# Neighbourhood attention on one core: where G's first tile, band 2's copies and band 3's loads stand in the order

## The chip, the cores and the metric

The kernel runs on one core of a Trainium2 chip. A core has five engines that each work through a queue of their own in order: TensorE (PE, matrix products into PSUM), VectorE (DVE), ScalarE (ACT), GpSimd (POOL) and SyncE (SP), which issues most of the DMAs. They wait for each other by semaphores. The time is that of one execution on the device, in microseconds; of several runs the median is given.

## The reference, cut to what matters

The image x has 224 x 224 pixels of 192 channels in bf16. Each pixel attends to 49 others: a 7 x 7 grid with a step of two pixels, clipped at the borders of the image.

```python
qkv = x @ wqkv                                   # 192 -> 3 * 192
off = jnp.arange(7) * 2
r0 = jnp.clip(ir - 6, 0, H - 1 - 12); c0 = jnp.clip(ic - 6, 0, W - 1 - 12)
nidx = rows r0 + off, columns c0 + off           # 49 neighbours of each pixel
logits = einsum('bnc,bnkc->bnk', q, k[nidx]) * C ** -0.5
p = softmax(logits)
o = einsum('bnk,bnkc->bnc', p, v[nidx]) @ wo
```

## The kernel before

**Pixels.** Because the step of the grid is two, a pixel meets only rows and columns of its own parity. The rows are handled in 14 steps n, each of one row parity rc and one group ti of 16 rows of it (`steps`, L591), and each step in seven pairs m = 0 to 6 of two slots of 8 columns (`pairs`). So there are 98 pairs, k = 0 to 97. Both column parities (cc) of a slot are done together.

**Algebra.** q and k are not formed. The scores are x times G, where G is x times the product of the two weight matrices (AW); V is x times the product of wv and wo (WP, WB). G and V are made one step ahead: while step n attends, PE makes G and V for step n + 1.

**Input.** x is loaded as 14 bands of 16 image rows. `load_items` (L145) issues three transposing DMAs on SP for one band: channels go to the partitions, two tiles into the rings XA[0] and XA[1], and a third into a tile X1 with 64 rows of either column parity. X1 has two buffers, so X1 of band b takes the buffer of X1 of band b - 2 once all readers of that are done. `xb_items` (L158) copies the halves of X1 into the rings XB[0] and XB[1], whose other 64 partitions hold marks that mask what lies outside of the grid. `sort_items` (L167) copies a band from XA and X1 into XS in the order that V needs. Later bands are copied and sorted by POOL, through the list `pool_q`.

**One pair.** `stage1` multiplies G by the x rows of a slot (PE, L499) into one of two standing PSUM tiles, SS[0] for slot 0 and SS[1] for slot 1, and takes the negative maximum nmx (DVE, L501). `stage1b` makes the exponentials p (ACT, L508), two instructions a slot. `stage2` transposes p (PE, L527; called T below) and copies the result out of PSUM (DVE, L528). `stage3` multiplies by V (PE, L537, into o_ps). `stage4` divides by the sum (DVE, L543 and L560) and stores. The stages of pair k are interleaved with the later stages of pairs k - 1 and k - 2.

**Work for the next step.** For G there are four column groups (`GROUPS`), each with three items (`g_items`): two `whole` tiles, one for each column parity (PE L417, then copied to G by `evac`, on ACT L330), and one `halves` item that goes by ACT to a tile gx and from there by POOL (L452) into G. There are 14 V items (`v_item`: PE L337 and L340, then ACT L330 or DVE L328). All these PSUM tiles come from one pool of three banks (`ps_g`), so a fourth waits until the first is copied out.

**The order.** The order on each engine is that of the program text (`in_order`, L90). In the main loop (L657) a pair emits the scores of both slots, the exponentials of slot 0, stage 3 and the first stage 4 of pair k - 2, then the list `w64`, the exponentials of slot 1, stage 2 of pair k - 1, the second stage 4, one load (`ld.pop`, L700), and the list `w128`. In steps 1 to 12 w64 is a `halves` item in even pairs and empty in odd pairs; w128 holds one `whole` tile (two in pair 1) and two V items. In step 0 the order of this later part is written out by hand in `PLAN` (L606), one string a pair: V is a V item of step 0, W one of step 1, G and H `whole` tiles of steps 0 and 1, X a copy of band 2 into XB, R and T copies of V between its two buffers by DMA (`v_over`), N the second stage 4; a or d behind it names ACT or DVE.

**Around the change in step 0.** `load_items(2)` is issued before the loop (L628). SP then carries, in order, `g_row_on(0, 4, 10)` (L278), a first load of band 3, the v copy R-:0:8, a second load of band 3, R-:8:14, `first_vd` (L366), `g_row_on(1, 2, 12)`, `g_col_on` (L284), the last load of band 3 (X1), and the stores of pairs 2 and on. POOL sorts bands 1 and 2 in pairs 0, 1 and 3 and copies band 3 into XB from pair 4 on.

Of the kernel before, what the change touches and what calls it, by code (L numbers as in the profile page):

```python
# [19 lines left out]
S = 112  # L20
# [3 lines left out]
NBAND = 14  # L24
# [43 lines left out]
def _win(t, p0, pn, off, dims):  # L68
    a = t[:]
    ps = a.ap[0][0]  # L70
    return bass.AP(a.tensor, a.offset + p0 * ps + off, [[ps, pn]] + [list(d) for d in dims])
# [28 lines left out]
def kernel(  # L100
# [7 lines left out]
    nc = tc.nc  # L108
# [19 lines left out]
    XB = [pers.tile([128, RP * RW], BF, name=f"xb{m}") for m in range(2)]  # L128
    XDAT = (0, 64)
# [8 lines left out]
    X1 = {}  # L138
# [6 lines left out]
    def load_items(b):  # L145

        src = xp[16 * b:16 * b + 16].rearrange("r j c -> (r j) c")
        at = (16 * b) % (2 * RP) * S

        def one(k):  # L150
            if k == 1:
                X1[b] = x1_p.tile([128, BND], BF, name=f"x1_{b}", tag="x1")
            dst = X1[b][:] if k == 1 else XA[k // 2][:, at:at + BND]
            nc.sync.dma_start_transpose(out=dst.unsqueeze(1), in_=src[:, 128 * k:128 * k + 128])  # L154

        return [lambda k=k: one(k) for k in ((0, 2, 1) if b in (0, 2, 3) else (1, 0, 2))]

    def xb_items(b, eng):  # L158
        at = (16 * b) % (2 * RP) * S
        return [lambda m=m: eng(out=XB[m][XDAT[m]:XDAT[m] + 64, at:at + BND], in_=X1[b][XDAT[m]:XDAT[m] + 64, :]) for m in range(2)]  # L160
# [45 lines left out]
    for cc in range(2):  # L206
        t = pers.tile([128, S], BF, name=f"ch{cc}")
        at = (S - KS) % MM if cc else 0
# [65 lines left out]
    def g_row_on(rc, s0, ns):  # L274

        for cc in range(2):
            p = XROW[cc]
            nc.sync.dma_start(out=_win(G[rc][cc], p, 32, (NSLOT + s0) * 128, [[128, ns], [1, 128]]), in_=_win(G[rc][cc], p, 32, (NSLOT + 1) * 128, [[0, ns], [1, 128]]))  # L278
# [63 lines left out]
    def v_item(rc, ti, cb):  # L342
        def emit(dve):
            pv = ps_g.tile([128, 512], F32, name="pv", tag="pg")
            v_mms(pv, lambda k, h: XS[rc][:, k, cb, 64 * h:64 * h + 64])
            evac(_win(VV[rc][ti % 2], 0, 128, AT[cb] * VP, [[193, 2], [1, C]]), pv[:, 0:2 * C].rearrange("p (t c) -> p t c", c=C), dve)
        return emit

    def v_over(rc, ti, c0, c1, eng=nc.sync):

        eng.dma_start(out=VV[rc][1 - ti % 2][0:64, c0:c1, 0:VP - 1], in_=VV[rc][ti % 2][0:64, c0:c1, 0:VP - 1])
# [153 lines left out]
    def stage1b(J, ab):  # L505
        s_ps, nmx = J.s[ab]
        for cc in range(2):
            nc.scalar.activation(out=J.p[:, ab, cc].rearrange("p q (r k) -> p q r k", k=8), in_=_win(s_ps, 0, 128, cc * 256, [[8, 2], [16, 16], [1, 8]]),  # L508
                                 func=ACTF.Exp, bias=nmx[:, cc:cc + 1], scale=1.0)
# [20 lines left out]
    def stage3(J, ab):  # L530
        rc, s = J.rc, 2 * J.m + ab
        o_ps = (ps_o if J.k < NP - 1 else ps_g).tile([128, 512], F32, name="o_ps", tag="o" if J.k < NP - 1 else "pg")
        V = (VV[rc][1 - J.ti % 2], VV[rc][J.ti % 2])
        for cc in range(2):
            for q in range(2):
                for h in range(2):
                    nc.tensor.matmul(o_ps[64 * h:64 * h + 64, cc * 193:cc * 193 + 193], lhsT=J.pt[:, 4 * ab + 2 * cc + q, 64 * h:64 * h + 64],  # L537
                                     rhs=V[h][:, AT[(s - 1 + q) % NSLOT], cc * C:cc * C + 193], start=(q == 0), stop=(q == 1))
        J.o_ps[ab] = o_ps

    def stage4a(J, ab):
        J.rs[ab] = stat.tile([128, 2], F32, name="rs", tag="rs")
        nc.vector.reciprocal(out=J.rs[ab][:], in_=J.o_ps[ab][:, C:C + 2])  # L543
        return J.rs[ab]
# [55 lines left out]
    def g_all(n):  # L600
        ti, rc = steps[n]
        its = [g_items(rc, ti, s0, ns) for (s0, ns) in GROUPS]
        return [it for (w0, w1, h) in its for it in (w0, w1)], [h for (w0, w1, h) in its]

    act, dve, pool = nc.scalar.copy, nc.vector.tensor_copy, nc.gpsimd.tensor_copy
    PLAN = (  # L606
        "Va:0 Vd:1 Va:2 Vd:3 Va:4 Vd:5 Va:6 Vd:7 R-:0:8 Va:8 Gd:2 Ga:3 X-",
        "Va:9 Vd:10 X- Va:11 Vd:12 Va:13 R-:8:14 Gd:4 Ga:5",
        "Gd:6 N- Ga:7 Wa:0 Wd:1 Wa:2",
        "Hd:0 N- Ha:1 Wa:3 Wa:4 Wd:5",  # L610
        "Hd:2 N- Ha:3 Wa:6 Wa:7 Ta:0:8 Wd:8",
# [37 lines left out]
    g_row(1, 0, 0, 1, pool, first1)  # L649
    g_row(1, 0, 1, 1, pool, first1)  # L650
    g_row_on(0, 4, 10)
    xb2 = xb_items(2, dve)

    v0 = [v_item(0, 0, cb) for cb in (13, 0, 1, 2, 3, 4, 5, 6, 7, 8, 9, 10, 11, 12)]
    ld = []
# [1 line left out]
    for k in range(NP + 2):  # L657
        J = pairs[k] if k < NP else None
        n = J.n if J else NSTEP
        w64, w128 = [], []  # L660
        if J:
            m = J.m
            if m == 0 and n + 1 < NSTEP:
                ti1, rc1 = steps[n + 1]
                gw, gh = g_all(n + 1)
                vs = [v_item(rc1, ti1, cb) for cb in (0, 1, 2, 3, 4, 5, 6, 13, 7, 8, 9, 10, 11, 12)]
            if n == 0:
                w64 = (gh0 + gh)[m + 1:m + 2]
            elif n + 1 < NSTEP:
                w128 = gw[m + (m > 1):m + 1 + (m > 0)] + vs[2 * m:2 * m + 2]  # L670
                w64 = gh[m // 2:m // 2 + 1] if m % 2 == 0 else []
            stage1(J, 0)
            stage1(J, 1)
            stage1b(J, 0)
            if m == 0 and n + 3 < NBAND:
                ld = load_items(n + 3)
        if k == NP:
            stage2(pairs[k - 1])
        if k >= 2:
            stage3(pairs[k - 2], 0)  # L680
            stage3(pairs[k - 2], 1)
            if k >= NP:
                stage4a(pairs[k - 2], 0)
                stage4a(pairs[k - 2], 1)
            stage4(pairs[k - 2], 0)
            if k == NP - 1:
                stage4a(pairs[k - 2], 1)
        for it in w64:
            it(False)
        if J:  # L690
            stage1b(J, 1)
        if 1 <= k < NP:
            stage2(pairs[k - 1])

        if k >= 2 and n > 0:
            stage4(pairs[k - 2], 1)
        if not J:
            continue

        if ld:  # L700
            ld.pop(0)()
        for w in PLAN[m].split() if n == 0 else ():
            (kind, by), at = w.split(":")[0], [int(c) for c in w.split(":")[1:]]
            if kind in "VWGH":
                {"V": v0, "W": vs, "G": gw0, "H": gw}[kind][at[0]](by == "d")
            elif kind == "N" and k >= 2:
                stage4(pairs[k - 2], 1)
            elif kind == "X":
                xb2.pop(0)()
            elif kind == "R":  # L710
                v_over(0, 0, at[0], at[1], nc.scalar if by == "a" else nc.sync)
            elif kind == "T":
                v_over(rc1, ti1, at[0], at[1], nc.scalar if by == "a" else nc.sync)
        for it in w128:
            it(False)
            if it is vs[7]:
                v_over(rc1, ti1, 0, 8)
            if it is vs[13]:
                v_over(rc1, ti1, 8, 14)
        if n == 0 and m == 0:  # L720
            for q in range(2):
                marks(q, 2 * MM, 2 * MM + 3, pool)
        if n == 0 and m == 1:
            first_vd()
            g_row_on(1, 2, 12)
            g_col_on()
        if n == 0 and m >= 3:
            marks_on(m % 2, 2 * MM + 3 + (m - 3) // 2)
        add = []
        if n == 0:  # L730
            add = {0: sort_items(1, 1, pool), 1: sort_items(2, 1, pool), 3: sort_items(2, 0, pool), 4: xb_items(3, pool) + sort_items(3, 0, pool)}.get(m, [])
        else:
            if m == 0 and n + 2 < NBAND:
                add = sort_items(n + 2, J.rc, pool)

            if m in ((2, 4) if n > 1 else (3,)) and n + 3 < NBAND:
                srt = sort_items(n + 3, J.rc, pool)
                one, two = xb_items(n + 3, pool) + srt[2:], srt[:2]
                add = (two if m == 4 else one) if n > 1 else one + two
        pool_q[:0] = add  # L740
        if n == 1 and m == 1:
            g_col(0, 1, 0, 1, pool)
            g_row(0, 1, 0, 1, pool, ((0, 16, MM - 6, 1),))
            g_row(0, 1, 1, 13, pool, ((0, 6, MM - 6, 1),))
        if n == 12 and m == 1:
            last = ((0, 9, 0, 1), (9, 7, 9, 0))
            g_col(1, 6, 0, 1, pool)
            g_row(1, 6, 0, 1, pool, last)
            g_row(1, 6, 1, 13, pool, last[1:])
        pool_do(5 if n == 1 and m == 3 else 4)  # L750
# [34 lines left out]
```

## Time and profile before

| | us |
|---|---|
| median of three runs | 362.62 (361.67, 362.62, 364.1) |
| the profiled execution | 363.39 |
| its span on the core | 361.6 |
| PE busy | 335.6 |
| DVE busy | 322.0 |
| ACT busy | 318.7 |
| POOL busy | 278.8 |

A row of the timeline gives the start of an instruction (or of several alike in a row) from the span's start, how long it or they took, the engine, the line, the operation, the tile written and the tile read, the shapes and the count; in brackets stands how long the engine was idle before it, and what ended that. SPq marks an instruction of SP's queue. A row of the windows gives, for a stretch, its length and then the busy time and number of instructions of PE, PE's weight loads, DVE, ACT and POOL, then the clock granted to PE as a share of full speed, the share of the DMA engines and GB/s. The maxima (L501) mark the pairs: in the steady part a step takes 22.8 us, and a pair 3.0 to 3.6.

### The profile page before, as it was taken

The numbers are of one execution on the slowest core, as the hardware profiler recorded it, in microseconds if no ns is written. First come the engines' busy times: TensorE is split into PE (matmuls) and PEld (weight loads), VectorE is DVE, ScalarE is ACT, GpSimd is POOL, SyncE is SP. The second block draws the span as 40 slices with busy tenths as digits, with TensorE's granted clock in tenths as the row PEclk, the third lists the DMA queues.
The fourth block names the chain that finished last, engine by engine and source line by source line (L and its number), as shares of the span: only waits on it lengthen the run. The fifth ranks groups of instructions, "written<-read, shape, count | busy, mean of one in ns | idle before, by whom it ended". The sixth has DMA issues, their size and how long they took to land.

```text
span 361.6 us, 19886 instructions
## 1 busy us (share of the span) xinstructions
PE 335.6 (93%) x8374; PEld 302.6 (84%) x8374; DVE 322.0 (89%) x743; ACT 318.7 (88%) x825; POOL 278.8 (77%) x442
## 2 busy tenths in 40 slices
PE   4686999999999999999999999999999999999882
PEld 2565878897998999999889899898999999888772
DVE  8877999988999999999899998999989889889893
ACT  7854779998999989999999999999999899899792
POOL 8395799999998959959699696896978866474082
PEclk9998999999999999999999999999999999999998
DMA  9997866798959889597785977949869535425423
GB/s 192 205 177 107 169 135 145 159 171 168 181 128 175 146 161 172 123 175 149 153 179 114 179 157 152 172 111 180 166 133 175 122 71 118 98 53 114 97 68 88
DMA packets 125446, 51.85 MB, mean 143 GB/s; under 512 B 88131, under 2 KB 124832, under 8 KB 125357
## 3 DMA queue, kind: packets, MB, share of 16 engines
q1 hardware_dynamic: 118564, 47.79, 67.5%
q0 software_dynamic: 5280, 1.71, 2.8%
q10 hardware_dynamic: 1512, 1.10, 1.6%
q8 instruction: 65, 1.06, 1.2%
q14 instruction: 25, 0.20, 0.2%
HBM read 0.29 MB, written 19.27 MB: 54 GB/s over the span
## 4 chain that ended last, share of the span: by engine, by line
PE 61%; ACT 10%; POOL 10%; DVE 8%; issue 4%; SPq 3%; DMA 1%; DVEq 0%; ACTq 0%; POOLq 0%
PE s L499 14%; PE o_ps L537 12%; PE pg L417 9%; PE pt_ps L527 8%; PE pv L337 7%; ACT p L508 7%; PE pv L340 7%; PE pgh L417 5%; DVE nmx L501 4%; POOL xs L170 3%; SPq L154 3%; POOL out_dram L589 2%; POOL xb L160 2%; DVE pt_sb L528 1%; POOL g L452 1%
## 5 line engine op out<-in xcount | busy, mean ns | idle before, releaser
L508 ACT ACTIVATE p<-s,nmx 128x256 bf16<-128x256 f32 x392 | 160.3, 476 | 27.6 <-DVE nmx L501 26.7
L501 DVE TENSOR_REDUCE nmx<-s 128x2 f32<-128x448 f32 (+1 forms) x196 | 113.9, 623 | 16.3 <-PE s L499 14.2
L452 POOL COPY g<-gx 64x512 bf16<-64x512 bf16 (+1 forms) x110 | 62.1, 564 | 52.5 <-ACT gx L330 49.0
L560 DVE TENSOR_TENSOR o_sb<-o_ps,rs 128x384 bf16<-128x384 f32 x169 | 94.2, 558 | 7.3 <-DMA out_dram<-o_sb 1.5
L589 POOL DMA_DIRECT2D out_dram<-o_s x150 | 84.3, 569 | 10.1 <-DVE rs L543 8.5
L330 ACT CAST v<-pv 128x384 bf16<-128x384 f32 x193 | 87.7, 525 | 2.9 <-PE pv L340 2.7
L499 PEld LDWEIGHTS <-g 128*64 128x64 bf16 x2640 | 84.5, 110 | 3.5 <-issue 2.2
L537 PE MATMUL o_ps<-v,pt_sb 128*64 128x193 bf16 x1568 | 85.2, 246 | 2.3 <-ACT pt_sb L528 2.0
L499 PE MATMUL s<-xa,g 128*64 128x196 bf16 (+9 forms) x1320 | 82.2, 218 | 1.6 <-ACT p L508 1.2
L499 PE MATMUL s<-xb,g 128*64 128x196 bf16 (+9 forms) x1320 | 81.7, 217 | 0.2 <-ACT g L330 0.2
L337 PE MATMUL pv<-wb,xs 128*64 128x384 bf16 x406 | 71.3, 333 | 10.5 <-DVE xs L362 3.9
L537 PEld LDWEIGHTS <-pt_sb 128*64 128x64 bf16 x1568 | 69.7, 109 | 3.7 <-ACT pt_sb L528 2.7
L340 PE MATMUL pv<-wp,xs 128*64 128x192 bf16 x812 | 72.2, 250 | 0.6 <-issue 0.4
L340 PEld LDWEIGHTS <-xs 128*64 128x64 bf16 x812 | 57.1, 111 | 11.5 <-issue 1.1
L528 DVE COPY pt_sb<-pt_ps 128x1024 bf16<-128x1024 bf16 x92 | 63.1, 686 | 1.1 <-PE pt_ps L527 0.9
L527 PE MATMUL pt_ps<-ident,p 128*64 128x128 bf16 x1552 | 62.3, 219 | 0.1
L330 ACT CAST g<-pg 128x512 bf16<-128x512 f32 (+4 forms) x136 | 57.5, 470 | 2.9 <-PE pg L417 2.8
L527 PEld LDWEIGHTS <-p 128*64 128x64 bf16 x1552 | 55.5, 110 | 5.4 <-issue 0.3
L417 PEld LDWEIGHTS <-aw 128*64 128x64 bf16 x1320 | 52.7, 111 | 4.7 <-issue 1.0
L417 PE MATMUL pg<-xb,aw 128*64 128x512 bf16 (+9 forms) x440 | 53.2, 271 | 0.0
L417 PE MATMUL pg<-xa,aw 128*64 128x512 bf16 (+9 forms) x440 | 51.4, 272 | 0.3 <-DMA xa<-in_x_dram 0.3
L170 POOL COPY xs<-xa 128x896 bf16<-128x896 bf16 x51 | 46.0, 928 | 6.9 <-DMA xa<-in_x_dram 5.5
(73 smaller groups left out, 311.3 us busy)
## 6 DMA issues: line engine op xcount, KB each, us to landing
out_dram<-o_sb SPq DMA_DIRECT2D x156, 96.0 KB
v<-v SPq DMA_DIRECT2D x13, 385.0 KB
v<-v SPq DMA_DIRECT2D x13, 288.8 KB
out_dram<-o_s POOLq DMA_DIRECT2D x78, 9.0 KB, 3.4
out_dram<-o_sb SPq DMA_DIRECT2D x13, 78.0 KB
out_dram<-xs SPq DMA_DIRECT2D x13, 78.0 KB
v<-v SPq DMA_DIRECT2D x2, 337.8 KB
xa<-in_x_dram SPq DMA_TRANSPOSE x28
```

The lines of the kernel that those rows point to most:

```text
L330: nc.scalar.copy(out=out_, in_=in_)
L337: nc.tensor.matmul(pv[64 * h:64 * h + 64, 0:2 * C], lhsT=at(1, h), rhs=WB[:].rearrange("p t c -> p (t c)"), start=True, stop=False, skip_g ...
L340: nc.tensor.matmul(pv[64 * h:64 * h + 64, cc * C:(cc + 1) * C], lhsT=at(2 * cc, h), rhs=WP[(cc, 0)], start=False, stop=True, skip_group_ch ...
L417: nc.tensor.matmul(o, lhsT=l, rhs=r, start=(pas == 0), stop=(pas == 1))
L499: nc.tensor.matmul(o, lhsT=w, rhs=r, start=(cc == 0 and done[h] == cols_), stop=(cc == 1 and not units[h]), skip_group_check=True)
L501: nc.vector.tensor_reduce(out=nmx[:], in_=_win(s_ps, 0, 128, lo, [[256, 2], [16, 16], [1, 16 - lo]]), axis=AX.XY, op=ALU.max, negate=True)
L508: nc.scalar.activation(out=J.p[:, ab, cc].rearrange("p q (r k) -> p q r k", k=8), in_=_win(s_ps, 0, 128, cc * 256, [[8, 2], [16, 16], [1, ...
L527: nc.tensor.transpose(pt_ps[64 * h:64 * h + 64, 4 * ab + 2 * cc + q, :], J.p[:, ab, cc, q, 64 * h:64 * h + 64], ident[:])
L528: (nc.scalar.copy if J.n == NSTEP - 1 and J.m < 5 else nc.vector.tensor_copy)(out=J.pt[:], in_=pt_ps[:])
L537: nc.tensor.matmul(o_ps[64 * h:64 * h + 64, cc * 193:cc * 193 + 193], lhsT=J.pt[:, 4 * ab + 2 * cc + q, 64 * h:64 * h + 64], rhs=V[h][:, A ...
L560: nc.vector.tensor_tensor(out=o_sb[:], in0=_win(o_ps, 0, 128, 0, [[194, 2], [1, C]]), in1=rs[:].unsqueeze(2).to_broadcast([128, 2, C]), op ...
L589: pool_q.append(lambda dst=dst, p=p, m=n * nj, cc=cc: nc.gpsimd.dma_start(out=dst.rearrange("j i c -> i j c"), in_=o_sb[p:p + m, cc, :]))
```

## The change

Four edits:

1. Band 2's three loads are issued with X1 first, then XA[0] and XA[1]; before X1 came last.
2. Band 2's two copies into XB, on DVE in pairs 0 and 1 of step 0 (the entries X in PLAN), become two DMAs on SP, issued ahead of the loop behind `g_row_on(0, 4, 10)`.
3. In step 0 the three loads of band 3 are spread over pairs 1, 2 and 3; before over 0, 1 and 2.
4. In the odd pairs of steps 1 to 12 the first `whole` tile of G moves from w128 to w64: on PE ahead of stage 2's transposes, and on ACT between the exponentials of slot 0 and those of slot 1.

```diff
-        return [lambda k=k: one(k) for k in ((0, 2, 1) if b in (0, 2, 3) else (1, 0, 2))]
+        return [lambda k=k: one(k) for k in ((0, 2, 1) if b in (0, 3) else (1, 0, 2))]
...
-        "Va:0 Vd:1 Va:2 Vd:3 Va:4 Vd:5 Va:6 Vd:7 R-:0:8 Va:8 Gd:2 Ga:3 X-",
-        "Va:9 Vd:10 X- Va:11 Vd:12 Va:13 R-:8:14 Gd:4 Ga:5",
+        "Va:0 Vd:1 Va:2 Vd:3 Va:4 Vd:5 Va:6 Vd:7 R-:0:8 Va:8 Gd:2 Ga:3",
+        "Va:9 Vd:10 Va:11 Vd:12 Va:13 R-:8:14 Gd:4 Ga:5",
...
-    xb2 = xb_items(2, dve)
+    for q in range(2):
+        p, at = XDAT[q], 32 * S
+        nc.sync.dma_start(out=_win(XB[q], p, 64, at, [[256, 7], [1, 256]]), in_=_win(X1[2], p, 64, 0, [[256, 7], [1, 256]]))
...
-                w64 = gh[m // 2:m // 2 + 1] if m % 2 == 0 else []
+                w64 = gh[m // 2:m // 2 + 1] if m % 2 == 0 else [w128.pop(0)]
...
-            if m == 0 and n + 3 < NBAND:
+            if m == (1 if n == 0 else 0) and n + 3 < NBAND:
                 ld = load_items(n + 3)
```

## The prediction

> **What bounds the kernel now.** I read the page's busy times first, then the timeline of each engine in step 0 and in one step of the steady part (step 7, from 195 us), then the windows and the waits.
>
> ```profile
> PE 335.6 (93%) x8374; PEld 302.6 (84%) x8374; DVE 322.0 (89%) x743; ACT 318.7 (88%) x825; POOL 278.8 (77%) x442
> ```
>
> Three engines near 90% say only that no single one is free. The stages differ. In steps 1 to 12 PE issues without a hole in nearly every pair. In step 0 all three wait; here are the DVE, PE and windows rows of pair 1.
>
> ```profile
> 25.53 3.04 DVE L160 COPY xb<-x 64x1792 bf16<-64x1792 bf16 x1
> 28.50 1.17 DVE L501 TENSOR_REDUCE nmx<-s 128x2 f32<-128x480 f32 x2
> 30.53 0.35 PE L337 MATMUL pv<-wb,xs 128*64 128x384 bf16 x2 [2.22 <-ACT gx L330]
> 31.64 0.53 PE L337 MATMUL pv<-wb,xs 128*64 128x384 bf16 x2 [0.59 <-ACT v L330]
> 28.20:31.60 3.40, 0.64 (x10) 0.33 (x6) 3.37 (x6) 2.43 (x7) 1.00 (x2) 0.97 1.21 150
> 31.60:35.00 3.40, 3.35 (x39) 2.68 (x40) 1.28 (x3) 0.97 (x3) 3.18 (x4) 0.52 0.14 31
> ```
>
> The first copy of band 2 into XB takes 3.04 us on DVE; the median of the six DVE copies of this line is 0.624. POOL's three sorts run from 25.41 to 28.09 beside it. The maxima of pair 1 stand behind it, then the exponentials, then gx, whose bank PE needs: 2.22 us of idle PE. In the next 3.4 us the granted clock (the number after the five engines) is 0.52.
>
> After that two queues carry the load. POOL is busy 40.52 of the 42 us from 40 to 82, without a gap from 44.23 on, and the chain that ended last runs through it there (xs, xb, out). Its first work that needs band 3, and the SP rows ahead of it:
>
> ```profile
> 33.68 0.63 SPq L351 DMA_DIRECT2D v<-v  x1
> 34.35 1.97 SPq L366 DMA_DIRECT2D v<-v  x2
> 36.42 3.71 SPq L278 DMA_DIRECT2D g<-g  x2
> 40.18 2.18 SPq L284 DMA_DIRECT2D g<-g  x2
> 42.46 1.69 SPq L154 DMA_TRANSPOSE x<-in_x_dram  x1
> 44.26 3.73 SPq L566 DMA_DIRECT2D out_dram<-o_sb  x4
> 49.29 3.39 POOL L160 COPY xb<-x 64x1792 bf16<-64x1792 bf16 x2
> ```
>
> SP never stops here. X1 of band 3 is issued at 42.46 and its burst on the DMA engines ends at about 46.4 (busy slices of the window 40 to 50), 4.0 us later.
>
> The steady part, ACT and PE rows of pairs 3 and 4 of step 7, and PE in pair 1:
>
> ```profile
> 206.08 1.57 ACT L508 ACTIVATE p<-s,nmx 128x256 bf16<-128x256 f32 x4
> 207.52 0.60 ACT L330 CAST g<-pg 128x512 bf16<-128x512 f32 x1
> 209.80 0.58 ACT L330 CAST gx<-pgh 128x512 bf16<-128x512 f32 x1
> 210.28 0.84 ACT L508 ACTIVATE p<-s,nmx 128x256 bf16<-128x256 f32 x2
> 208.04 0.27 PE L499 MATMUL s<-xa,g 128*64 128x196 bf16 x3
> 200.35 0.37 PE L337 MATMUL pv<-wb,xs 128*64 128x384 bf16 x2
> 201.09 0.35 PE L337 MATMUL pv<-wb,xs 128*64 128x384 bf16 x2 [0.20 <-ACT g L330]
> ```
>
> The odd pair 3 runs its four exponentials in a row (206.08), then G; the even pair 4 has gx between (209.80), as the change will have in odd pairs. 208.04 is where the second slot's scores of pair 4 start on PE. In pair 1 the second V item waits for a bank that G's first tile still holds.
>
> **The copies of band 2.** Removed: two DVE copies. The second (30.76, 0.87 us) sits before 0.91 us of DVE idle: nothing. Without the first, the maxima start when slot 0's scores end, at about 26.45, not 28.50: 2.05 us. Everything through PE's 31.64 moves by that. PE's 2.2 us hole closes, so the window that precedes the slow clock is full, and the half clock from 31.6 to 35.0 should go too: V items 12 and 13, two G tiles and the scores' start took 3.4 us, about 2.0 at full speed, so 1.4 more. Pair 2's scores start at 31.15, not 34.59: 3.4 us.
>
> [...]
>
> Added: two SP DMAs of 64 partitions. No such copy is in the trace. Issue: 0.6 to 0.8 us each (SBUF copies, such as 33.68). Landing: 2.2 to 6.0 us (the stores' landing). XB's band 2 is first read by the G tiles of step 1 in pair 3, about 36 us; issued near 23.5 they land by 30 at worst. Cost nothing, and if SP is later by 1.5 us the v copy behind them (24.80) still lands before pair 2's outputs at 31.9.
>
> **The order of band 2's loads.** X1 of band 2 now goes first and takes the buffer of X1 of band 0, whose last reader is the DVE sort that ends at about 14.96; SP is free at 13.75. SP waits 1.2 us, with band 2's other two transposes, the g copies of 20.77 and the v copy behind it; but the DMA engines still hold earlier transfers (the tile issued at 11.36 lands at 16.67), so they do not idle. Band 2 is first used by POOL at 29.8. Taken as 0; bounds 0 and 1.2 at pair 0, which waits for band 1 only.
>
> **Band 3 a pair later.** The v copy at 33.68 waits for V item 13; it moves to 30.85, 2.83 us earlier. Behind it stay 34.35, 36.42, 40.18; then the second transpose of band 3 (issued at 25.52 before; 1.69 by the row at 42.46, 1.8 with the gaps), and three stores (2.8 us of the four at 44.26) now precede X1 of band 3. Its issue: 42.46 - 2.83 + 1.8 + 2.8 = 44.2, landing at 48.2. POOL is ready at 49.29 - 3.4 = 45.9, waits 2.3 us there, with band 3's sorts and the copies of gx queued behind, and starts 1.1 us earlier than before. POOL has no gap to make this up until 111 us, and PE meets it at the V items of step 2 (82 us). So of 3.4 us **1.1** is kept. Bounds: 3.4 if the transpose lands in time, 0 if it lands at 49.3.
>
> **The odd pairs.** Steps 1 to 12, pairs 1, 3, 5. Nothing is added; T moves behind G on PE, exp of slot 1 behind G on ACT. T ends 0.05 late for DVE's copy, less than the wait below.
> - Pair 1: G's first tile is evacuated before the exponentials of slot 1, so its bank is free. The second V item follows the first by 0.33 elsewhere (207.05, 207.38), by 0.74 here: **0.41** gained; 0.48 of DVE and 0.43 of ACT idle behind it move along. In step 12, with five pieces of G, PE's pair is 4.12 long instead of 3.64: 0.9.
> - Pairs 3 and 5: the last exponential ended at 207.65 and now ends 0.48 later (209.80 to 210.28), at 208.13. Scores of slot 1 start at 208.04, so they wait 0.09 plus a handover of 0.05 (gx ended at 30.48, PE went at 30.53): 0.14. PE is packed, so it is lost: **0.28** a step.
> Net -0.13 in steps 2 to 11, -0.6 in step 12: -1.9. Step 1 lies under POOL's bound: 0. Bounds of the wait: 0 and 0.4 (longest bank wait of PE on ACT's G).
>
> **Sum.** -1.1 - 1.9 = -3.0. The profiled execution took 363.39 (span 361.6 and 1.8 around it), so 360.4 there. The median of the three is 362.62, 0.8 lower; on it the forecast is **359.6 us**.
>
> **Rivals.**
> 1. The scores of slot 1 do not wait. For: slack is 0.40 by the rows and the shift 0.48, a close call. Against: in even pairs the same order leaves 0.28 only because gx lengthens PE's pair too. -0.41 x 10 - 0.9 - 1.1 = -6.1: 356.5. Chance 0.15.
> 2. The front gain is kept whole: X1 of band 3 lands by 46. For: SP has idle time from 28.94 to 33.68 today. Against: the v copy bars it. -3.4 - 1.9: 357.3. Chance 0.13.
> 3. It is lost whole: the transpose lands at 49.3, POOL waits 3.4. For: SP and DMA are dense from 34 to 60. -1.9: 360.7. Chance 0.12.
> 4. Slower: the wait moves into S. Each of the two waits a step costs 0.09 plus a long handover; at 0.4, 0.8 x 11 = 8.8 lost against 5.0 + 1.1 gained: +2.7, 365.3. It decides from 0.28 us a wait. For: PE packed, ACT and DVE within 10% of it. Against: the 0.05 handover. Chance 0.15. In step 2 PE may then stand idle about 2.2 us for POOL, and a second slow window would add 1.4: 366.7.
> 5. The forecast, 358.3 to 361.3: chance 0.45.
>
> **Numbers.** One per cent (3.6 us) is about what a measurement can tell. Faster by more than that (below 359.0): rivals 1 and 2 and a quarter of 5, 0.39. Slower (above 366.2): a third of rival 4, 0.05. Within: 0.56. The range 356.9 to 364.2 leaves out about half of 1 and half of 4.
>
> **What would show it.** No L160 row on DVE after 13 us; pair 1 of step 0 with no PE idle above 1 us and the clock at 1.0 through 35 us; scores of pair 2 at 31.2. POOL L160 near 48.2 with an idle before it that ends with a DMA. In step 7: no wait for G in pair 1, PE's S waiting for ACT's p in pairs 4 and 6 by 0.1 to 0.2, a step of 22.6 instead of 22.78. The forecast is wrong if POOL's row stands at 46 or 49.3, or if the steps grow.

## The result, and the profile after

The changed kernel takes 366.42 us in the median of its runs (362.38 to 367.96), beside 362.94 for the kernel before: a ratio of 1.0071, with an interval of 1.0048 to 1.0095. The ratio leaves out the three runs above 367.8 us, the profiled one among them, as possibly disturbed; a second profile below, of 365.86 us, shows the same wait. The forecast was 359.6, so even the sign is wrong. In a second session, with four runs of the changed kernel, the ratio was 1.0142 (1.0108 to 1.0175). The runs of the changed kernel fall into two groups, one of 361.9 to 362.9 us (five runs) and a larger one of 365.3 to 368.2 us (18 runs; two of the 25 lie between), and the difference between the two is what this section is about; the kernel before has no such groups (360.3 to 365.1 over all its runs).

The profiled execution took 367.82 us (span 366.0), one of the larger group. The busy times, from the page:

```profile
PE 338.3 (92%) x8374; PEld 304.6 (83%) x8374; DVE 322.2 (88%) x741; ACT 321.1 (88%) x825; POOL 279.3 (76%) x442
```

PE's busy time is 2.7 us longer at the same number of matmuls, so PE ran slowly somewhere. DVE has two instructions less: the copies of band 2.

**Step 0 went as forecast.** No L160 row is left on DVE between 18 and 36 us. PE's idle rows around pair 1, and the windows that the forecast showed of before, here of after:

```profile
29.61 0.35 PE L337 MATMUL pv<-wb,xs 128*64 128x384 bf16 x2 [0.26 <-ACT gx L330]
30.73 0.35 PE L337 MATMUL pv<-wb,xs 128*64 128x384 bf16 x2 [0.60 <-ACT v L330]
```

```profile
28.20:31.60 3.40, 2.54 (x54) 2.09 (x50) 2.08 (x5) 2.81 (x7) 1.86 (x3) 1.00 1.15 189
31.60:35.00 3.40, 3.40 (x87) 2.93 (x83) 2.88 (x7) 2.42 (x6) 2.05 (x3) 1.00 0.52 89
```

The idle of 2.22 us is 0.26, and the second window, which had a clock of 0.52, has 1.00. From pair 0's maxima to pair 1's it now takes 7.35 us instead of 9.32, from there to pair 2's 5.44 instead of 6.84: 1.97 and 1.40 less, where 2.05 and 1.4 were forecast. Pair 0 itself came 1.0 us later (20.20 instead of 19.18), so the times below are to be read with about 1 us taken off.

**Then 6.4 us went in one pair.** From pair 0 to pair 1 of step 1 it takes 9.48 us instead of 3.07. The rows of SP, ACT, POOL and PE there:

```profile
42.45 2.78 SPq L566 DMA_DIRECT2D out_dram<-o_sb  x3
45.34 4.23 SPq L154 DMA_TRANSPOSE x<-in_x_dram  x1
...
45.96 0.69 ACTq L351 DMA_DIRECT2D v<-v  x1
...
46.31 0.60 POOL L566 DMA_DIRECT2D out_dram<-o_sb  x1
54.38 3.39 POOL L160 COPY xb<-x 64x1792 bf16<-64x1792 bf16 x2 [7.47 <-DMA x<-in_x_dram]
...
57.82 0.22 PE L417 MATMUL pgh<-xb,aw 128*64 128x48 bf16 x2 [1.82 <-POOL xb L160]
62.42 0.53 PE L337 MATMUL pv<-wb,xs 128*64 128x384 bf16 x1 [3.35 <-POOL xs L170]
```

SP issues the transpose of X1 of band 3 at 45.34, POOL is free at 46.91 and waits 7.47 us, until 54.38: the transpose landed 9.0 us after its issue. PE waits twice for what POOL makes from it. During the second wait the slow clock comes back (the matmul of L337 takes 0.53 instead of 0.35; in the windows the granted clock, the number after the five engines, falls from 1.00 to 0.61):

```profile
57.60:61.00 3.40, 1.25 (x33) 0.94 (x32) 1.33 (x3) 1.50 (x6) 3.28 (x6) 1.00 0.67 154
61.00:64.40 3.40, 1.98 (x27) 1.98 (x29) 0.00 (x0) 0.94 (x2) 3.36 (x6) 0.61 0.46 113
```

A landing is counted here, and below, up to the last of the sixteen steps by which a DMA raises its semaphore; in each of the six profiles in which POOL waits for this load, POOL starts 0.05 to 0.06 us after that last step (here it comes at 54.32). Before, the packets of the same transpose, issued at 42.46, ended 3.9 us after the issue, fifteen steps came by 47.04 and the last at 48.32, 5.9 us after the issue; POOL was busy until 49.29 and did not notice.

What is new in the changed kernel is the row between: ACT issues the v copy T:0:8 (385 KB) at 45.96, 0.62 us behind the transpose. Before, ACT issued it 5.84 us behind, when the transpose's packets had ended:

```profile
48.30 0.69 ACTq L351 DMA_DIRECT2D v<-v  x1
```

The DMA packets of the changed kernel by queue (number, MB, share of the 16 engines; queue 1 is SP's, queue 10 ACT's), from 47 to 50 us and from 50 to 53 us:

```profile
q10 hardware_dynamic: 467, 0.36, 66.2%
q1 hardware_dynamic: 125, 0.07, 9.8%
...
q1 hardware_dynamic: 2160, 0.64, 140.4%
q10 hardware_dynamic: 61, 0.04, 6.0%
```

From 47 to 50 us the engines carry ACT's copy above all, and the transpose's packets follow from 50 us on.

**The odd pairs.** Step 7 of after, ACT and PE where pair 3's exponentials of slot 1 meet pair 4's scores:

```profile
210.98 0.59 ACT L330 CAST g<-pg 128x512 bf16<-128x512 f32 x1
211.46 0.85 ACT L508 ACTIVATE p<-s,nmx 128x256 bf16<-128x256 f32 x2
...
212.13 0.25 PE L499 MATMUL s<-xb,g 128*64 128x112 bf16 x2
212.36 0.28 PE L499 MATMUL s<-xa,g 128*64 128x112 bf16 x3
```

The exponentials end at 212.31, the scores of slot 1 start at 212.36: the order and the 0.05 us between them are those of the wait that was forecast, and the pairs grow by about as much. Pairs 3 to 4 and 5 to 6 take 3.13 instead of 3.01, pair 1 to 2 takes 3.21 instead of 3.60, and the step 22.70 instead of 22.78.

### The profile page after: what moved, and what is told of

It is laid out like the page before. It is cut to its first block, busy times and chain, and to the rows that moved or that the text cites. A ratio compares the mean times of both kernels' runs of the same rounds, so it can differ in the third digit from the quotient of the medians.

```text
span 366.0 us, 19889 instructions
## 1 busy us (share of the span) xinstructions
PE 338.3 (92%) x8374; PEld 304.6 (83%) x8374; DVE 322.2 (88%) x741; ACT 321.1 (88%) x825; POOL 279.3 (76%) x442
## 3 DMA queue, kind: packets, MB, share of 16 engines
q0 software_dynamic: 5280, 1.71, 2.8%
## 4 chain that ended last, share of the span: by engine, by line
PE 74%; POOL 10%; DVE 6%; ACT 4%; issue 4%; DVEq 0%; POOLq 0%; ACTq 0%
PE s L499 17%; PE o_ps L537 15%; PE pg L417 11%; PE pt_ps L527 9%; PE pv L337 9%; PE pv L340 8%; PE pgh L417 5%; POOL xs L170 3%; ACT p L508 3%; POOL out_dram L589 2%; POOL xb L160 2%; POOL g L452 2%; DVE nmx L501 1%; POOL out_dram L566 1%; ACT pt_sb L528 1%
## 5 line engine op out<-in xcount | busy, mean ns | idle before, releaser
L508 ACT ACTIVATE p<-s,nmx 128x256 bf16<-128x256 f32 x392 | 165.1, 478 | 24.3 <-DVE nmx L501 23.4
L452 POOL COPY g<-gx 64x512 bf16<-64x512 bf16 (+1 forms) x110 | 62.0, 564 | 49.3 <-ACT gx L330 45.3
L499 PEld LDWEIGHTS <-g 128*64 128x64 bf16 x2640 | 86.4, 111 | 6.1 <-issue 3.1
L499 PE MATMUL s<-xa,g 128*64 128x84 bf16 (+7 forms) x1320 | 85.3, 218 | 2.3 <-ACT p L508 1.2
L499 PE MATMUL s<-xb,g 128*64 128x84 bf16 (+7 forms) x1320 | 84.7, 218 | 0.2 <-ACT g L330 0.2
L337 PE MATMUL pv<-wb,xs 128*64 128x384 bf16 x406 | 71.9, 335 | 9.8 <-DVE xs L362 3.7
L330 ACT CAST g<-pg 128x512 bf16<-128x512 f32 (+4 forms) x136 | 58.6, 463 | 2.3 <-PE pg L417 2.2
L417 PE MATMUL pg<-xa,aw 128*64 128x512 bf16 (+9 forms) x440 | 52.2, 270 | 0.0
```

What stands on the lines that cost most here:

```text
L330: nc.scalar.copy(out=out_, in_=in_)
L337: nc.tensor.matmul(pv[64 * h:64 * h + 64, 0:2 * C], lhsT=at(1, h), rhs=WB[:].rearrange("p t c -> p (t c)"), start=True, stop=False, skip_g ...
L417: nc.tensor.matmul(o, lhsT=l, rhs=r, start=(pas == 0), stop=(pas == 1))
L452: nc.gpsimd.tensor_copy(out=G[rc][cc][p:p + 64, 1, s0:s0 + ns, :], in_=gx[p:p + 64, 0:ns * 128].rearrange("p (s q) -> p s q", q=128))
L499: nc.tensor.matmul(o, lhsT=w, rhs=r, start=(cc == 0 and done[h] == cols_), stop=(cc == 1 and not units[h]), skip_group_check=True)
```

## The experiments

**Theory A**: X1 of band 3 is late because ACT's v copy is issued right behind it, POOL stands, and POOL's chain carries the delay to step 2. **Rivals**: the odd pairs cost the time (B); the added DMAs and band 2's order make SP late (C); a transpose at this place is slow by itself (D); lateness alone is harmless (E). Ratios are to the kernel before in the same session.

### The odd pairs alone

```diff
-                w64 = gh[m // 2:m // 2 + 1] if m % 2 == 0 else []
+                w64 = gh[m // 2:m // 2 + 1] if m % 2 == 0 else [w128.pop(0)]
```

> The kernel before with the odd pairs' G tile moved ahead, alone: loads and copies of bands 2 and 3 as before. Theory A (the loss lies at the load of band 3, the odd pairs do what was forecast): steps 2 to 11 shorter by about 0.1 us each, step 0 and the front of step 1 as before, so 1 to 2 us less than before (ratio 0.995 to 0.997). Rival B (the odd pairs cost time, which the trace of the changed kernel hides): pairs 3 and 5 wait more than 0.28 us each, steps longer than 22.78, ratio 1.005 or more. Step 11 was 1.0 us longer in the changed kernel (24.72 against 23.73): if that belongs to this edit it is seen here again.

Measured: 361.67 us beside 362.23, ratio 0.9989 (0.9965 to 1.0012). The steps are those of the changed kernel (22.69 to 22.71 in steps 3, 6, 7, 9), so B falls for the odd pairs as a whole. The gain is smaller than the 1 to 2 us expected: steps 3 to 9 together take 159.92 instead of 160.03 us. Step 11 is long again (24.78), but so it is in the next experiment (24.75), where the odd pairs are untouched: it does not belong to this edit.

This profile also showed that the front of the kernel before varies. Here pair 0's maxima came at 20.10, and DVE's copy of band 2 cost far less:

```profile
26.44 1.83 DVE L160 COPY xb<-x 64x1792 bf16<-64x1792 bf16 x1
...
30.23 0.35 PE L337 MATMUL pv<-wb,xs 128*64 128x384 bf16 x2 [1.00 <-ACT gx L330]
```

PE stood 1.00 us and not 2.22, the clock stayed at 1.00, and step 0 took 35.44 us instead of 38.09 with the copy still on DVE.

### Band 2 by DMA alone, band 3 as early as before

```diff
-        return [lambda k=k: one(k) for k in ((0, 2, 1) if b in (0, 2, 3) else (1, 0, 2))]
+        return [lambda k=k: one(k) for k in ((0, 2, 1) if b in (0, 3) else (1, 0, 2))]
...
-    xb2 = xb_items(2, dve)
+    for q in range(2):
+        p, at = XDAT[q], 32 * S
+        nc.sync.dma_start(out=_win(XB[q], p, 64, at, [[256, 7], [1, 256]]), in_=_win(X1[2], p, 64, 0, [[256, 7], [1, 256]]))
```

> The kernel before with band 2's copies into XB as two DMAs and X1 of band 2 loaded first; band 3 is loaded in pair 0 as before, the odd pairs are as before. Theory A (the loss is band 3's transpose, late behind ACT's v copy): X1 of band 3 is issued near 42 or earlier, lands before the v copy is issued, POOL starts its copies of band 3 without a wait or with less than 1 us of it near 46 to 47, and the time falls by 2 to 3.4 us against before (ratio 0.991 to 0.995). Rival C (the added DMAs or band 2's order of loads make SP's queue late by themselves): POOL's copies of band 3 wait 4 us or more, or pair 1 of step 0 is later than 28.5, ratio above 1.005.

Measured: 361.78 us beside 362.23, ratio 0.9988 (0.9971 to 1.0004). POOL starts its copies of band 3 at 47.49 without a wait, and pair 1 of step 2 has its maxima at 81.98 instead of 84.03. C falls. But less came out than expected, because step 0 lost 1.9 us in a new place, between pairs 2 and 3:

```profile
25.28 2.13 SPq L154 DMA_TRANSPOSE xa<-in_x_dram  x1
27.51 0.64 SPq L351 DMA_DIRECT2D v<-v  x1
...
33.58 0.86 PE L537 MATMUL o_ps<-v,pt_sb 128*64 128x193 bf16 x16 [1.71 <-DMA v<-v]
```

The first load of band 3 stands on SP ahead of the v copy R-:0:8 (27.51; it is 25.65 in the changed kernel), and pair 0's outputs, now earlier, wait 1.71 us for it. So, going by this one profile, loading band 3 a pair later does save something once step 0 is faster: it clears SP for this copy. The forecast had booked it as a cost only.

### The v copy moved from ACT to SP

The changed kernel with one word of the plan altered; SP then issues the copy behind the transpose, at 50.99.

```diff
-        "Hd:2 N- Ha:3 Wa:6 Wa:7 Ta:0:8 Wd:8",
+        "Hd:2 N- Ha:3 Wa:6 Wa:7 T-:0:8 Wd:8",
```

> The changed kernel with one edit: the v copy that ACT issues in pair 4 of step 0 (385 KB, its packets ran from 47.0 to 50.2 while the transpose of X1 of band 3, issued at 45.3, started at 49.9) is issued by SP, in whose queue it stands behind that transpose. Theory A (the transpose is late because ACT's copy got ahead of it): the transpose lands about 4 us after its issue, near 49 to 50, POOL waits 2 to 3 us for it instead of 7.5, the slow-clock window at 62.4 goes, and the time is 359 to 361.5 (ratio to before 0.99 to 0.997). Rival D (a transpose at this place is slow for another reason: the stores of SP's own queue, or its source): it still lands 8 to 9 us after issue, ratio 1.005 or more as in the changed kernel. The v copy itself lands later by some us; its reader is in step 1, so that should cost nothing under both.

```profile
44.56 1.96 SPq L154 DMA_TRANSPOSE x<-in_x_dram  x1
...
49.61 3.39 POOL L160 COPY xb<-x 64x1792 bf16<-64x1792 bf16 x2 [3.63 <-DMA x<-in_x_dram]
```

The transpose lands 5.0 us after its issue and POOL waits 3.63. The time is 361.77 us beside 362.23 (360.72 to 363.45 in ten runs; the group above 365 is gone), ratio 1.0003 (0.9983 to 1.0022). The same transpose in the same place, with the same stores around it, is 4 us faster once ACT's copy does not follow it: D falls. That the time only comes back to that of before, and not to 360, is a matter of the other terms (below).

### Band 3 a pair later, alone

```diff
-            if m == 0 and n + 3 < NBAND:
+            if m == (1 if n == 0 else 0) and n + 3 < NBAND:
```

> The kernel before with band 3's loads a pair later, alone; band 2's copies stay on DVE and the odd pairs as before. Theory A (lateness of X1 of band 3 is the whole loss): X1 of band 3 is issued about 46 to 47.5, less than 2 us before ACT's v copy (48.3); if the copy gets ahead the landing is 8 to 9 us after issue, near 55, POOL waits 6 to 9 us from about 46 to 49, and the time rises by 6 to 10 us (ratio 1.015 to 1.03); if the transpose keeps its 4 us it lands near 51, costing about 2 us (ratio 1.005). Rival E (the late load is not what costs, it is its meeting with the earlier front): no change, ratio 0.998 to 1.002.

> The kernel before with band 3's loads a pair later, once more, for a second profile. Its first profile (363.3 us) had the transpose issued 1.9 us ahead of ACT's v copy and landing 4.1 us after its issue, while most of its runs took 365 to 368 us. Theory A: in a profile above 365 us the transpose lands 7 us or more after its issue, with the v copy's packets ahead of it; in one below 364 it lands in 4 to 5. Rival: the wait is as short in a slow profile, and the time lies elsewhere.

Measured: 365.58 us beside 362.23 (363.3 to 368.55), ratio 1.0095 (1.0057 to 1.0133). So this edit alone makes a loss of the size of the whole change's, without a faster front, and E falls. The two profiles, of executions of 363.3 and 364.01 us, both show a quick transpose, the first issued 1.90 us ahead of the v copy, the second 0.99:

```profile
46.27 1.49 SPq L154 DMA_TRANSPOSE x<-in_x_dram  x1
...
48.17 0.68 ACTq L351 DMA_DIRECT2D v<-v  x1
...
50.36 3.39 POOL L160 COPY xb<-x 64x1792 bf16<-64x1792 bf16 x2 [1.26 <-DMA x<-in_x_dram]
```

```profile
45.61 1.49 SPq L154 DMA_TRANSPOSE x<-in_x_dram  x1
...
46.60 0.68 ACTq L351 DMA_DIRECT2D v<-v  x1
...
49.79 3.39 POOL L160 COPY xb<-x 64x1792 bf16<-64x1792 bf16 x2 [2.25 <-DMA x<-in_x_dram]
```

They land 4.0 and 4.1 us after issue. No execution above 365 us of this kernel was profiled, so that its long ones are long for the same reason is likely but not shown. The granted clock of its runs points that way: it was 0.985 to 0.988 in the four above 366 us and 0.992 to 0.998 in the three below 364, as a further slow window would have it.

### The changed kernel, profiled twice more

> The changed kernel once more, unaltered, beside the next two on one chip, with a second profile. Theory A (the transpose of X1 of band 3 is late when ACT's v copy gets ahead of it): a profile of about 366 us or more has the landing 8 to 9 us after the issue, POOL's wait of some 7 us and the slow clock behind it; a profile near 362.5 us has the transpose ahead of the v copy, a landing 4 to 5 us after issue and a wait of 2 to 4 us. Rival (the times differ for another reason, such as the clock at the start): the wait is the same 7 us whatever the time.

> The changed kernel a third time, for a profile. Theory A as before: near 362.5 us the transpose of X1 of band 3 lands 4 to 5 us after its issue and POOL waits 2 to 4 us; at 366 or more it lands after 8 to 9 and POOL waits about 7.

The second profile is of an execution of 365.86 us, the third of one of 361.89, the quick group (the kernel before took 361.93 beside it, one run of each):

```profile
44.19 1.42 SPq L154 DMA_TRANSPOSE x<-in_x_dram  x1
...
44.51 0.69 ACTq L351 DMA_DIRECT2D v<-v  x1
...
52.62 3.39 POOL L160 COPY xb<-x 64x1792 bf16<-64x1792 bf16 x2 [7.17 <-DMA x<-in_x_dram]
```

```profile
44.90 1.42 SPq L154 DMA_TRANSPOSE x<-in_x_dram  x1
...
45.75 0.68 ACTq L351 DMA_DIRECT2D v<-v  x1
...
49.17 3.39 POOL L160 COPY xb<-x 64x1792 bf16<-64x1792 bf16 x2 [2.49 <-DMA x<-in_x_dram]
```

One and the same program: with the v copy 0.32 us behind the transpose the landing takes 8.4 us, with 0.85 us it takes 4.2. Three profiles, two of the larger group and one of the quick one, fit the reading that the two groups of runs are the two outcomes. The profiles in which POOL waits for this load, and that of before, in one table (times in us; the last two columns test the second half of theory A):

| kernel | transpose issued | ACT's v copy behind it by | landed after | POOL's XB copies | maxima of pair 1, step 2 | from copies to maxima |
|---|---|---|---|---|---|---|
| before | 42.46 | 5.84 | 5.9 (no wait) | 49.29 | 84.03 | 34.7 |
| after, 367.82 us | 45.34 | 0.62 | 9.0 | 54.38 | 88.63 | 34.3 |
| after, 365.86 us | 44.19 | 0.32 | 8.4 | 52.62 | 86.88 | 34.3 |
| after, 361.89 us | 44.90 | 0.85 | 4.2 | 49.17 | 83.34 | 34.2 |
| band 3 late, first | 46.27 | 1.90 | 4.0 | 50.36 | 84.93 | 34.6 |
| band 3 late, second | 45.61 | 0.99 | 4.1 | 49.79 | 84.42 | 34.6 |
| v copy on SP | 44.56 | on SP, later | 5.0 | 49.61 | 83.77 | 34.2 |

In these rows POOL's copies fix the time up to pair 1 of step 2 within 0.6 us, so the forecast's reading of POOL's chain was right. In the four other profiles with X1 last, the v copy follows by 5.0 to 7.2 us and the landing takes 4.4 to 5.7.

### X1 of band 3 loaded first

The kernel with the v copy on SP, and X1 as the first of band 3's loads.

```diff
-        return [lambda k=k: one(k) for k in ((0, 2, 1) if b in (0, 3) else (1, 0, 2))]
+        return [lambda k=k: one(k) for k in ((0, 2, 1) if b == 0 else (1, 0, 2))]
```

> The changed kernel with the v copy of step 0's pair 4 on SP and band 3's loads in the order of band 2's: X1 goes first, in pair 1 of step 0. It then takes the buffer of X1 of band 1, whose last reader on POOL ends at about 28.0, so SP waits some 2 us there, and X1 lands near 31 to 33; the other two are issued near 40 and 45 and land by 49.5, when POOL wants them. Theory A (POOL's wait for X1 is what the front of step 1 pays, and POOL's chain sets the time up to pair 1 of step 2): POOL starts the XB copies of band 3 without a wait near 46, pair 1 of step 2 has its maxima 34.2 to 34.5 us later, near 80.5 instead of 83.8, and the time falls by about 3 us against the kernel with only the v copy moved: 358 to 359.5, ratio to before 0.988 to 0.993. Rival G (PE, not POOL, is the bound by then): pair 1 of step 2 stays within 1 us of 83, 361 or more. Rival H (SP's wait makes the v copy at 32.1 late and PE's outputs of step 0 wait for it): step 0 longer than 35 by 1 us or more.

Measured: 361.5 us beside 362.16, ratio 0.9989 (0.9969 to 1.001): a miss. X1 was issued at 28.45, and POOL started at 46.66 without a wait, as expected, but pair 1 of step 2 has its maxima at 82.57, 35.9 us after the copies: the next limit stood close behind. Pairs 5 and 6 of step 1 take 4.37 and 4.07 us instead of 3.1 and 3.5:

```profile
74.66 0.56 DVE L560 TENSOR_TENSOR o_sb<-o_ps,rs 128x384 bf16<-128x384 f32 x1 [1.29 <-DMA out_dram<-o_sb]
```

DVE waits for one of the six output buffers, whose store has not landed: in step 1 SP carries stores, copies of marks, the v copies and band 4's loads nearly without a pause. The mechanism that this run was to show (POOL's wait gone) is there, its price was not got, since another wait took its place.

### G first in pair 1 only

On top of the last kernel: pairs 3 and 5 go back to the old order.

```diff
-                w64 = gh[m // 2:m // 2 + 1] if m % 2 == 0 else [w128.pop(0)]
+                w64 = gh[m // 2:m // 2 + 1] if m % 2 == 0 else [w128.pop(0)] if m == 1 else []
```

> The kernel with X1 first, and G's first tile ahead of the exponentials in pair 1 only, no longer in pairs 3 and 5. Theory A (pairs 3 and 5 each lose 0.12 us because the scores of slot 1 wait for the exponentials that now come later, and PE has no slack to take it up): pairs 3 to 4 and 5 to 6 take 3.01 again, the steps of 22.70 become 22.46, and the time falls by 2.4 to 2.7 us against the kernel with X1 first: 355.5 to 357. Rival I (what is saved there is lost in the pair behind, since ACT is the bound): steps of 22.65 to 22.75 and no difference.

Measured: 359.18 us beside 362.16, ratio 0.9927 (0.9902 to 0.9952). Pairs 3 to 4 and 5 to 6 take 3.01 again, the step 22.42 instead of 22.70, and steps 3 to 9 take 157.74 instead of 159.87: the waits of 0.12 were lost time. The expectation's total (355.5 to 357) counted on the gain that the kernel with X1 first had not brought; the difference between the two, 2.3 us, is close to the 2.4 to 2.7 expected. The wait for output buffers, 2.8 us in all before this edit, grew:

```profile
DVE o_sb L560 <- DMA out_dram<-o_sb: 5.2, 4, 2.1
```

### Nine output buffers instead of six

```diff
-            o_sb = work.tile([128, 2, C], BF, name="o_sb", tag="o_sb", bufs=6)
+            o_sb = work.tile([128, 2, C], BF, name="o_sb", tag="o_sb", bufs=9)
```

On top of the last kernel, and on the kernel before:

> The kernel with X1 first and G first in pair 1 only, with nine buffers instead of six for the output tile that DVE writes (o_sb). In that kernel DVE waited four times, 5.2 us in all and 2.1 at most, for a buffer whose store had not landed; in the kernel before it waited twice, 1.5 in all. Theory (what the front gained in step 0 is partly given back in step 1 because the stores on SP's queue are late there and the output buffers run out): the waits go, step 1 shrinks from 25.9 to 23 or less, and the time falls by 1 to 3 us, to 356 to 358, ratio to before 0.983 to 0.99. Rival J (SP's queue is itself the bound in step 1, buffers or not, or POOL's chain is next at 34.3 us from the XB copies to pair 1 of step 2): the wait moves to another place and the time stays within 1 us of 359.2.

> The kernel before with nine buffers for the output tile instead of six, nothing else. Theory (the output buffers ran out only because step 0 ended earlier and POOL no longer waited): its two waits, 1.5 us in all, lie near 73 us and late, and taking them away is worth 0 to 1.5 us, ratio 0.996 to 1.0. Rival K (the buffers are a limit of the kernel before as well, whatever is done at the front): 3 us or more, ratio 0.992 or less.

With it the last kernel takes 356.78 us beside 362.43, ratio 0.9842 (0.9809 to 0.9876): it beats both kernels. The waits for output buffers are gone and step 1 takes 22.42 us instead of 25.89. The kernel before gains nothing from it: 362.04 beside 361.88, ratio 0.999 (0.9963 to 1.0017). The buffers became a limit only when the front was faster.

### Pair 1's order alone, on the kernel before

```diff
-                w64 = gh[m // 2:m // 2 + 1] if m % 2 == 0 else []
+                w64 = gh[m // 2:m // 2 + 1] if m % 2 == 0 else [w128.pop(0)] if m == 1 else []
```

> The kernel before with G's first tile ahead of slot 1's exponentials in pair 1 alone, nothing else. Theory (pair 1 gains 0.39 us in steps 2, 3, 6 to 9, some 0.23 in steps 4, 5, 10, 11 and nothing in step 12; what pairs 3 and 5 lost is gone): steps of 22.42 instead of 22.78, 2.5 to 3.5 us less, ratio 0.990 to 0.994. Rival I (ACT is the bound, the gain is lost in the next pair): 1 us or less, ratio 0.997 or more.

Measured: 359.2 us beside 361.88, ratio 0.9908 (0.9874 to 0.9941), with steps of 22.42 us. One of edit 4's three pairs is worth more than all four edits.

## Why the prediction was wrong

**The step that failed: "Band 3 a pair later".** Its first half held. The issue of X1 was put at 44.2 and came at 45.34, 44.3 with pair 0's lateness taken off; POOL was ready at 46.91, 45.9 by the same count, as forecast. The second half, "landing at 48.2", took the 4.0 us of before's row for this place. It measured 9.0 and 8.4 us in two profiles, and 4.2 in the third. In before ACT's v copy did not follow until 5.84 us later. Counted from pair 0's maxima, the edits bring that copy forward by 3.4 us and put the transpose back by 1.9, so the gap shrank to 0.3 to 0.9 us. The 4.0 was also the end of the packets and not of the wait: by the last step of the semaphore before's row gives 5.9, with which the landing comes at 50.1 and nothing of the front gain is kept even without a collision. The forecast counted every DMA that the transpose moved past on SP's own queue, and none on ACT's. It named "SP and DMA are dense from 34 to 60" for a loss of the front gain only (rival 3, up to 49.3); a landing at 54.4 was outside all its cases. It cost 5.3 us at pair 1 of step 2 between two profiles of the same program (88.63 against 83.34); 5.2 of them are POOL's later copies.

**Its rival that was slower** (the wait moves into S) ended near the result, at 365.3, for another reason: the handover was 0.05 us, as the forecast itself took it, and the odd pairs cost nothing in sum. That its number is near is luck. Its last sentence, PE idle for POOL and a second slow window, did name what came, but as a remark on step 2 and on odd pairs that take longer: it came in step 1, from the late transpose.

**The front.** Right in mechanism and size for the front that the profile of before shows: 1.97 and 1.40 us against 2.05 and 1.4. But in two of six profiles with the copy on DVE, step 0 was 35.4 and 35.7 us long instead of 38.1 to 38.4, since pair 0 came some 1 us later and DVE's copy then began later and was shorter. When pair 0 comes goes with the clock of PE at the start: in all fourteen profiles the V matmuls begin at 11.56 to 11.59, but the clock comes to full between 14.2 and 17.4, and pair 0's maxima are at 18.7 to 19.2 where it does so by 14.7 and at 19.7 to 20.2 from 16.5 on. The forecast took one execution for the rule. Where the wait was long (2.22 us of idle PE, then a clock of 0.52), the 1.40 us of clock went with it. How much of the gain would be kept behind POOL was put at 1.1 us; with the transpose quick it was 0.69 (84.03 against 83.34) and 0.26 (83.77, v copy on SP), or 1.5 and 0.4 counted from pair 0's maxima.

**The odd pairs.** Pair 1 in steps 3 and 6 to 9: 0.39 gained against 0.41. Pairs 3 and 5: 0.12 lost in each against 0.14, by the wait named. The sum was mis-sized, -1.9 against about -0.3 us. In steps 4 and 5 pair 1 gains only 0.24 and 0.22 (3.36 and 3.38 instead of 3.60), and these steps take 0.05 and 0.16 us more than before (23.11 and 23.20 against 23.05 and 23.04, the quick profile beside that of before); steps 3 to 9 together gain 0.24 (159.79 against 160.03), where 0.91 was forecast. In step 12, -0.6 was forecast: the gain of pair 1 was read from a profile in which it took 4.08 from pair 1 to pair 2; of four other profiles with the old order two show 4.08 and two show 3.80 to 3.81, and with the new order it is 3.80 to 3.81 each time. At best 0.28 is gained there, which the two waits take back: the step takes 23.51 to 23.55 with edit 4 and 23.23 to 23.82 with the old order. What makes steps 4 and 5 different was not followed up.

**The costs booked at nothing** (the two DMAs into XB, the order of band 2's loads) were nothing: 0.26 us of PE idle in pair 1, no wait for XB in step 1 other than band 3's. Pair 0's maxima come at 18.8 to 20.2 us in the eight profiles with band 2's new order and at 18.7 to 20.1 in the six with the old.

**The sum.** Without the collision, -1.1 and -1.9 become about -0.3 to -0.7 and -0.3: the quick profile, 361.89, lies 1.5 us below the profile of before (0.69 of it by pair 1 of step 2, 0.34 in steps 10 to 12, where times vary anyway), though level with the one run of before beside it, and the kernel with the v copy on SP is level with before. With the collision the larger group of runs lies 4.4 us above the quick one (366.9 against 362.5 in the mean).

## What to carry to other kernels

When an edit brings one stage forward and another transfer back, list what every queue issues around the transfer's new time, not only its own: a landing time read from a profile holds for its neighbours there (the same transpose landed 5.9 us after its issue in before, and after 9.0, 8.4 and 4.2 in the three profiles of the changed kernel). Read it up to the last step of the semaphore that the consumer waits for, not to the end of the packets (5.9 us against 3.9 in the profile of before). A reordering that gains in one place and waits in two is worth trying place by place, since here the one place that gained was worth 2.7 us and all three together nothing that was clear of noise. When a wait is removed and the time does not move, look at which engine waits next and for what: here buffers that had been deep enough for the slower front.

## What was not expected of the hardware

- **A transpose was held up by a copy issued after it on another queue.** 0.32 and 0.62 us ahead of the v copy it landed after 8.4 and 9.0 us, 0.85 us and more ahead after 4.0 to 5.9. It happened in two ways. In the profile of 367.82 us SP's issue itself took 4.23 us instead of 1.4 to 2.0, and the transpose's 256-byte packets began in number only at 49.9, when ACT's were nearly done. A long issue next to such a copy is not peculiar to two queues: in eleven profiles SP issues a transpose of band 3 about 0.7 us behind its own v copy of the same 385 KB, and that issue takes 3.1 to 4.0 us each time, where the median of the other 487 transposes after 15 us, in all profiles, is 1.85 and only eleven of them take 3.1 or more. In the profile of 365.86 us the issue took 1.42, the packets ran from 45.5 to 48.7, and POOL was still released only at 52.62: the semaphore's steps came from 49.76 to 52.57, among those of the v copy (50.14 to 51.95). In the quick profile the packets ended at 48.5, the steps came from 48.86 to 49.11, ahead of the v copy's, and POOL went at 49.17. In the profile of 365.86 us, then, the last of the transpose's packets had ended 3.9 us before POOL was released, and the steps came late, among the v copy's. What held them was not shown, and for the first case, the long issue, the cause stays open.
- **DVE's copy of band 2 ended when POOL's three sorts ended, whenever it started.** In six profiles it started between 25.08 and 26.44 us and took 3.20 to 1.83 us, and it ended at 28.27 to 28.57, each time 0.48 us after the sorts (27.80 to 28.09); the median copy of this line takes 0.62. An end that does not depend on the start reads as a wait: by these rows DVE stood through all that was left of the three sorts, also in the one profile in which its row starts first (25.08, the first sort at 25.12). What made it wait was not shown.
- **The clock of PE did not fall by the length of a single gap alone.** Single gaps of 2.22 to 2.38 us (four profiles with the copy on DVE) were followed by a stretch at half clock each time, single gaps of 1.00 to 1.71 us by none. But in the profile of 365.86 us the clock fell at 58.59, only 1.28 us into a gap, with another of 1.59 us shortly before. What fits all six falls in mid-kernel is a grid in stretches of 3.41 us, which is how long the half clock itself lasted in the profiles of before and of 367.82 us: they lie a whole number of them (5 or 13) after the clock first came to full (in the profile of before, full at 14.35 and half at 31.42, 17.07 later; in that of 367.82 us, full at 17.38 and half at 61.76, 44.37 later), and in the stretch just ahead of each PE was busy for 0.5 to 1.25 us. The sparsest stretches without a fall behind them have 1.6 and 1.7 us of PE's work. By this, an estimate from six falls, the same wait costs the clock or not by where it lies on the grid.
- **Single steps near the end vary by up to 1.3 us.** In steps 10 to 12 one pair or another takes 3.8 to 4.8 us instead of 3.3 to 3.6, with or without any of the edits, and step 11 takes 23.55 to 24.83. A pair's time there should not be read from one profile, as the forecast did in step 12.
